# Reloading one batch in another layout, and reordering the start of an attention-plus-Fourier kernel

## The chip, the cores and the metric

The kernel runs on one core of a Trainium2 chip, as one launch. The metric is the device time of that launch in microseconds (us), and the number before is the median of seven executions.

## The reference

For each of 8 batches and 8 heads, 512 rows of `x` and 32 rows of `state` (64 wide) attend to each other. The 544 result rows of a batch, heads side by side (512 wide), then go through a two-dimensional Fourier mix of which only the real part is kept, a normalisation, a two-layer network (512 to 2048 to 512, relu) and a residual:

```python
a  = softmax(scale * x @ state.T);   xread = a @ state      # 512 rows per head
a2 = softmax(scale * state @ x.T);   sread = a2 @ x         # 32 rows per head
x  = concat([xread, sread]) as (8, 544, 512)
u  = x + real(fft(fft(x, axis=1), axis=2))
un = (u - mean(u)) / sqrt(var(u) + 1e-6)
out = u + relu(un @ w_ch1) @ w_ch2
```

## The kernel before

**Stages.** Each batch passes through four stages, each of which is a list of small steps (Python closures that issue instructions when called). `attend(b)` gives the scores (TensorE matmuls into tiles `eTp` and `esp`, ScalarE exps into `ET` and `E`) and then the reads (`xrp`, `xfp`, `xlp`, `srp`), which VectorE divides into `XR`, `XF`, `XL` and folds into `XQ`. `transform(b)` is the Fourier mix as matmuls with cosine and sine tables (`gp`, then `yp`), the sum `U`, its statistics, the centred `ub` and its transpose `unT`. `layer1(b)` multiplies with `w1` into `ph` and applies relu into `hT`; for batch 0 it works in quarter steps L[0] to L[15], of which L[0] to L[3] use the first 128 columns of `unT` and one quarter of `w1` each. `layer2(b)` multiplies with `w2` into `po` and writes the output.

**Who sets the order.** The program order of all engines is written out by hand: what is called first is issued first, and each engine works through its own queue. The first batch and part of the second stand in an explicit list (lines 818 to 830 before the change); after that, `weave` (line 797) merges the step lists of a stage by a fractional position, given as (list, start, end) for each. Between the steps at the start stand dummy matmuls: `warm(n)` (line 806) issues n 128x128 matmuls of the identity with itself, and `warmed(steps, n)` puts n of them behind each step.

**Loads.** `load_x(b)` fills the tile `xs` (two buffers). For batches 0 and 1 (line 112) partition p holds rows 4p to 4p+3 of every head, four rows of 64 floats in one run of 1,024 bytes: "four-row packets". Other batches are loaded row by row, 256 bytes each, in six DMAs on SyncE's (SP's) queue (lines 122 to 130), one of which has 31 partitions and one a single partition. The row order differs between the two layouts, so batches 0 and 1 undo the four-row interleave in `scores_t` (line 413) with strided matmuls: 18 for each of two head groups. `cast_x(b)` turns `xs` into the bf16 tile `xin`. For batches 0 and 1 TensorE transposes `xin` into `xT`; for later ones the DMA engines do it.

The weights are loaded by GpSimd's (POOL's) queue: `w1` behind a small copy into `gate` that waits for batch 0's x (lines 300 to 302), `w2` in `last_loads` (line 323). `more_loads` (line 309) stands in the list of batch 0's transform: it waits for batch 0's `XQ`, casts batch 1's x, then at line 312 reads `xs` of batch 0 and the last quarter of `w1`, and only then are a state reversal in DRAM, the load of batch 2's x and the clears for odd batches (`clears(1)`) in line. `clears(i)` (line 288) zeroes the pad columns of `XF`, `XR` and `XL` and some other tiles.

The explicit list of the second part reads, as far as the change touches it:

```python
for step in (warmed(t0[:2], 2) + [alternate, more_loads] + warmed(t0[2:4], 2) + [last_sines, exp_again, last_loads, turned[2], load_x3,
        t0[4], t0[8], W(6), turns1, t0[5], W(10), t0[7], copies1[0], copies1[1], t0[6], copies1[2],
        L[0], s1[0], t0[9], L[1], t0[10], s1[1], L[2], t0[11], t0[12], L[3], s1[2], r1[0], L[4], s1[3],
```

Here `t0` are the steps of `transform(0)`, `s1` and `r1` the scores and reads of batch 1, `s1[0]` and `s1[1]` its `scores_t`, `turns1` its transposes and `copies1` the copies of those out of PSUM. `t0[9]` transposes `ub` (0,0), `t0[10]` makes `ub` (1,1) on ScalarE, and `t0[12]` transposes that one.

Of the kernel before, what the change touches and what calls it, by code (L numbers as in the profile page):

```python
# [30 lines left out]
def kernel(  # L31
# [8 lines left out]
    nc = tc.nc  # L40
    B, H, S, D = x.shape
# [7 lines left out]
    NM = 288  # L49
# [59 lines left out]
    def load_x(b):  # L109
        xs = wk.tile([128, 4 * dm], F32, name="xs", tag="xs")  # L110
        xs_of[b] = xs
        if b < 2:
            v = xs.rearrange("p (h r) -> p h r", h=H)
            xb = x[b].rearrange("h (p i) d -> p h (i d)", i=4)
            n = 2 if b == 0 else 4
            for h in range(0, H, n):
                queue = nc.scalar if b == 0 and h in (0, 4) else nc.sync
                queue.dma_start(out=v[:, h:h + n, :], in_=xb[:, h:h + n, :])
            return
        v = xs.rearrange("p (i h d) -> p i h d", i=4, d=D)  # L120
        xb = x[b].rearrange("h s d -> s h d")
        for ps, si, rows in (
            (slice(32, 128), 2, xb[288:384]),
            (slice(0, 128), 0, xb[1:129]),
            (slice(0, 128), 1, xb[129:257]),
            (slice(0, 128), 3, xb[384:512]),
            (slice(0, 31), 2, xb[257:288]),
            (slice(31, 32), 2, xb[0:1]),
        ):
            nc.sync.dma_start(out=v[ps, si], in_=rows)  # L130

    def cast_x(b, copy=nc.gpsimd.tensor_copy, lo=0, hi=H):
        if b < 2:
            copy(xin_bufs[b % 2][:, :, 1 + D * lo:1 + D * hi].rearrange("p i (h d) -> p h i d", d=D),
                 xs_of[b].rearrange("p (h i d) -> p h i d", i=4, d=D)[:, lo:hi])
        else:
            copy(xin_bufs[b % 2][:, :, 1:513], xs_of[b].rearrange("p (i c) -> p i c", i=4))  # L137

    load_state(0, 1)
    load_x(0)  # L140
    load_state(1, 2)
    load_x(1)


    def turn_in_dram(lo, hi):
        nc.sync.dma_start(out=s_dram[lo:hi].rearrange("b h j d -> (b h) j d"),
                          in_=state[lo:hi, :, ::-1, :].rearrange("b h j d -> (b h) j d"))
# [137 lines left out]
            nc.gpsimd.memset(TO[0:1, lo:lo + 256:2], -v)  # L285
            nc.gpsimd.memset(TO[0:1, lo + 1:lo + 256:2], v)

    def clears(i):
        nc.gpsimd.memset(XFs[i][:, :, 512:514], 0.0)
        nc.gpsimd.memset(XRs[i][:, :, 0:514:513], 0.0)  # L290
        nc.gpsimd.memset(XLs[i][:, 512:514], 0.0)
        if i == 0:
            nc.gpsimd.memset(XE[:, 2, :], 0.0)
            nc.gpsimd.memset(XO[:, 2, :], 0.0)
            nc.gpsimd.memset(XO[:, 0:2, 0:257:256], 0.0)
        nc.gpsimd.memset(XNs[i].rearrange("p a b -> p (a b)"), 0.0)

    nc.gpsimd.tensor_copy(gate, xs_of[0][:, 0:2048:512])  # L300
    for q in range(4):
        nc.gpsimd.dma_start(out=w1[:, :, q * 512:(q + 1) * 512], in_=w1v[:, :, q * 512:(q + 1) * 512])
# [6 lines left out]
    def more_loads():  # L309
        nc.gpsimd.tensor_copy(gate[:, 0:1], XQs[0][:, 3, 0, 0:1])  # L310
        cast_x(1)
        nc.gpsimd.tensor_tensor(gate, xs_of[0][:, 0:4], w1[:, :, 3 * 512], op=ALU.add)
        turn_in_dram(3, B)
        load_x(2)
        clears(1)
        nc.gpsimd.memset(stb[:, 2:].rearrange("p b g c -> p (b g c)").bitcast(F32), 0.0)
# [10 lines left out]
    def qt(name, dt=F32):  # L327
        return psQ.tile([128, 512 if dt == F32 else 1024], dt, name=name, tag="q")
# [29 lines left out]
    def attend(b):  # L358
# [6 lines left out]
        sT = wk.tile([128, 4, 128], BF16, name="sT", tag="sT")  # L365
        xT = wk.tile([128, 4, S], BF16, name="xT", tag="xT")
# [45 lines left out]

        def scores_t(g):
            p = qt("eTp")
            for i in range(4):
                x0 = 128 * i
                for cols, rows in ((slice((i - 1) % 4, 285 if i == 0 else 288, 4), slice(x0 + (i == 0), x0 + 72)),
                                   (slice(287, 288), slice(0, 1)) if i == 0 else (None, None),
                                   (slice(291 - i, S, 4), slice(x0 + 127, x0 + 71, -1))):
                    for hp in range(2 if cols else 0):  # L420
                        nc.tensor.matmul(p[:, cols], lhsT=sT[:, 2 * g + hp, :], rhs=xT[:, 2 * g + hp, rows],  # L421
                                         start=(hp == 0), stop=(hp == 1))
            nc.scalar.activation(ET[:, g, :], p, AF.Exp, scale=scale)


# [286 lines left out]
    def layer1(key):  # L712
        low = isinstance(key, tuple)
        n = 128 if low else 512
        hT = wk.tile([128, FC, n], BF16, name="hTL" if low else "hT", tag="hTL" if low else "hT", bufs=1 if low else 2)
        h_of[key] = hT
        per = 512 // n

        def step(i):
            ph = psF.tile([128, 512], F32, name="ph", tag="c")  # L720
            for f in range(per * i, per * i + per):
                o = (f % per) * n
                for c in range(DC):
                    nc.tensor.matmul(ph[:, o:o + n], lhsT=w1[:, c, f * 128:(f + 1) * 128], rhs=un_of[key][:, c, :],  # L724
                                     start=(c == 0), stop=(c == DC - 1))
            nc.scalar.activation(hT[:, per * i:per * i + per, :].rearrange("p a b -> p (a b)"), ph, AF.Relu,  # L726
                                 scale=-1.0 if key in flipped else 1.0)

        def quarter_step(i, r):
            ph = psF.tile([128, 512], F32, name="ph", tag="c")  # L730
            for f in range(4 * i, 4 * i + 4):
                o = 128 * (f % 4)
                for c in range(DC):
                    nc.tensor.matmul(ph[:, o:o + 128], lhsT=w1[:, c, f * 128:(f + 1) * 128],  # L734
                                     rhs=un_of[key][:, c, 128 * r:128 * r + 128], start=(c == 0), stop=(c == DC - 1))
            nc.scalar.activation(hT[:, 4 * i:4 * i + 4, 128 * r:128 * r + 128], ph.rearrange("p (a b) -> p a b", b=128),  # L736
                                 AF.Relu, scale=-1.0 if key in flipped else 1.0)

        if key == 0:
            return [lambda i=i, r=r: quarter_step(i, r) for r in range(4) for i in range(FC // 4)]  # L740
        return [lambda i=i: step(i) for i in range(FC // per)]
# [69 lines left out]
    def warmed(steps, n):  # L811
        return [lambda s=s: (s(), warm(n)) for s in steps if s is not None]

    warm(12)
    s0, r0 = attend(0)
    s1, reads_next = attend(1)
    t0 = transform(0)
    for step in warmed(s0[:1], 8) + warmed(s0[1:2], 6) + warmed(s0[2:3], 14) + [second_table] + warmed(s0[3:5], 4) + s0[5:]:
        step()
    weave((warmed(r0, 4), 0, 1), ([sines], 0.25, 0.25), ([more_sines], 0.3, 0.3), ([lambda: warm(44)], 1, 1))  # L820
    load_x3 = lambda: (load_state(3, B, s_dram), load_x(3))
# [1 line left out]
    L, M, r1, t1 = layer1(0), layer2(0), reads_next, transform(1)  # L823
    W = lambda n: (lambda: warm(n))
    turns1, copies1, s1 = s1[0], s1[1:4], s1[4:]
    for step in (warmed(t0[:2], 2) + [alternate, more_loads] + warmed(t0[2:4], 2) + [last_sines, exp_again, last_loads, turned[2], load_x3,
            t0[4], t0[8], W(6), turns1, t0[5], W(10), t0[7], copies1[0], copies1[1], t0[6], copies1[2],
            L[0], s1[0], t0[9], L[1], t0[10], s1[1], L[2], t0[11], t0[12], L[3], s1[2], r1[0], L[4], s1[3],
            r1[2], t0[13], L[5], r1[1], L[6], r1[3], L[7], r1[4], r1[5], L[8], r1[7],
            lambda: state_ones(2, B), lambda: [r() for r in first_roots], L[9], L[10]]):  # L830
        step()
# [3 lines left out]
    for b in range(1, B + 1):  # L835
        reads_next = reads_after
        l2, l2_now = (layer2(b), l2[10:]) if b == 1 else (layer2(b) if b < B else [], l2)
        streams = [(l2_now + (layer2(("L", b // 4)) if b in (3, 7) else []), 0, 1)]
        if b < B:
            streams.append((layer1(b), 0.13 if b == 2 else 0.08, 1))  # L840
        if b + 1 < B:
            streams.append((reads_next, 0, 0.34))
            streams.append((transform(b + 1), 0.47 if b == 1 else 0.4, 0.77 if b == 3 else 0.8))
        if b + 2 < B:
            scores_next, reads_after = attend(b + 2)
            streams.append(([lambda: (cast_x(b + 2), turned[b + 2]())], 0.2, 0.2))
            streams.append((scores_next, 0.5, 1))
        if b + 3 < B:
            streams.append(([lambda: load_x(b + 3)], 0.35, 0.35))
        if b in (3, 7):  # L850
            streams.append((low_rows(b // 4), 0.02, 0.2))
            streams.append((layer1(("L", b // 4)), 0.36, 0.8))
        weave(*streams)
# [30 lines left out]
```

The softmax here doesn't subtract the row's maximum and nothing guards it: scores larger than these inputs give would overflow.

## Time and profile before

| what | value |
|---|---|
| time, median of 7 runs (lowest to highest) | 313.33 us (313.14 to 313.9) |
| the profiled execution: its time, its span | 313.23 us, 311.5 us |
| TensorE matmul, busy | 298.2 us, 96% of the span |
| VectorE, busy | 184.1 us, 59% |
| ScalarE, busy | 135.0 us, 43% |
| GpSimd, busy | 73.3 us, 24% |
| dummy matmuls (`warm`, line 809), busy | 12.6 us, 144 of them |
| scores of batches 0 and 1 (`eTp`, line 421), share of the chain | 1% |
| batch x loads of 256 KB on SP, median from issue to landing | 4.7 us |
| weight loads of 512 KB on GpSimd's queue, median from issue to landing | 11.2 us |

How to read it: in the lines of the profile PE is TensorE's matmuls, PEld its weight loads, DVE VectorE, ACT ScalarE, POOL GpSimd and SP SyncE. An L with a number is a line of the kernel before. "Busy" counts dummies as work, so TensorE's share says how little it pauses, not how much of its work is needed. Matmul ends are modelled, so the distance from one start to the next is the surer measure. Idle time in brackets names what ended it.

### The profile page before, as it was taken

To read this page: it belongs to the slowest core of one execution; us is meant where nothing else is said; L and a number is where in the kernel's file an instruction comes from. 1 tells how busy PE (TensorE), PEld (TensorE's weight loads), DVE (VectorE), ACT (ScalarE), POOL (GpSimd) and SP (SyncE) were. 2 spreads that over 40 slices of the span, in tenths; PEclk is the share of its full clock that TensorE was granted. 3 is DMA by queue.
4 is the path that set the end of the run, shared out by engine and by line. 5 is a ranking of instruction groups with operands and counts; after the bars stand their busy time and mean duration, and the time that the engine had idled before them with its cause. 6 is when DMAs were issued, how large, how long until landed. Compare 5 with 4: busy or idle time off the path is not lost.

```text
span 311.5 us, 5999 instructions
## 1 busy us (share of the span) xinstructions
PE 298.2 (96%) x2316; PEld 172.6 (55%) x2348; DVE 184.1 (59%) x441; ACT 135.0 (43%) x265; POOL 73.3 (24%) x168
## 2 busy tenths in 40 slices
PE   5988999999999999999999999999999999999995
PEld 5867996544544545456545554455445544555443
DVE  8787782786878484864727684686469563100112
ACT  5598674736533443244533435244424333333300
POOL 5969590540240040301500024002200131000000
PEclk9999999999999999999999999999999999999999
DMA  7997999159255756267533579631333034303055
GB/s 243 196 182 134 176 149 203 44 120 190 48 116 96 145 104 136 71 115 122 136 95 54 128 122 163 135 86 51 85 70 67 36 83 97 76 34 67 36 131 138
DMA packets 108052, 34.86 MB, mean 112 GB/s; under 512 B 97400, under 2 KB 103800, under 8 KB 108024
## 3 DMA queue, kind: packets, MB, share of 16 engines
q1 hardware_dynamic: 98840, 28.72, 45.3%
q0 software_dynamic: 4224, 4.19, 8.5%
q10 hardware_dynamic: 4960, 1.57, 2.1%
q8 instruction: 18, 0.29, 0.4%
q14 instruction: 10, 0.08, 0.1%
HBM read 22.41 MB, written 14.02 MB: 117 GB/s over the span
## 4 chain that ended last, share of the span: by engine, by line
PE 82%; DVE 13%; issue 2%; ACT 2%; POOL 1%; DVEq 0%; POOLq 0%; ACTq 0%
PE po L789 32%; PE ph L724 30%; PE gp L599 4%; PE ph L734 3%; DVE U L569 2%; DVE st L335 2%; PE warm L809 1%; PE eTp L421 1%; PE po L781 1%; PE yp L565 1%; PE xfp L457 1%; PE xrp L457 1%; PE yp L564 1%; PE gp L603 1%; PE esp L432 1%
## 5 line engine op out<-in xcount | busy, mean ns | idle before, releaser
L789 PE MATMUL po<-w,hT 128*128 128x512 bf16 x476 | 122.0, 379 | 1.5 <-issue 0.8
L726 ACT ACTIVATE hT<-ph 128x512 bf16<-128x512 f32 x112 | 66.9, 597 | 124.8 <-PE ph L724 122.7
L724 PE MATMUL ph<-unT,w 128*128 128x512 bf16 x437 | 114.0, 379 | 1.0 <-DVE ot L755 0.3
L724 PEld LDWEIGHTS <-w 128*128 128x128 bf16 x576 | 51.1, 98 | 47.9 <-issue 0.8
L789 PEld LDWEIGHTS <-hT 128*128 128x128 bf16 x496 | 47.1, 98 | 45.3
L755 DVE SCALAR_TENSOR_TENSOR ot<-po,rstd,U 128x512 f32<-128x512 f32 (+2 forms) x33 | 24.2, 732 | 52.8 <-PE po L789 44.9
L609 POOL COPY GL<-G 128x128 bf16<-128x128 bf16 x8 | 2.3, 291 | 113.7 <-ACT G L607 113.7
L569 DVE TENSOR_TENSOR U<-yp,XR 128x512 f32<-128x512 f32 x16 | 10.9, 682 | 27.0 <-PE yp L565 27.0
L335 DVE BATCH_NORM_STATS2 st<-U 128x6 f32<-128x512 f32 x32 | 21.8, 682 | 0.1
L342 POOL TENSOR_TENSOR rstd<-rstd,mhalf 128x1 f32<-128x1 f32 x34 | 21.0, 619 | 2.7
L341 POOL TENSOR_TENSOR rstd<-mv,epst 128x1 f32<-128x1 f32 x34 | 6.8, 200 | 62.5 <-DVE mv L337 62.5
L607 ACT CAST G<-gp 128x288 bf16<-128x288 f32 x31 | 12.1, 397 | 10.7 <-PE gp L603 5.7
L734 PE MATMUL ph<-unT,w 128*128 128x128 bf16 x256 | 16.1, 219 | 0.5 <-ACT unT L645 0.5
L809 PE MATMUL warm<-ident 128*128 128x128 bf16 x144 | 12.6, 236 | 3.7 <-POOL ident masks.py:199 3.3
L734 PEld LDWEIGHTS <-w 128*128 128x128 bf16 x256 | 15.0, 98 | 0.8 <-issue 0.6
L599 PEld LDWEIGHTS <-XQ 128*128 128x128 bf16 x96 | 8.8, 98 | 8.8 <-DVE XQ L529 2.5
L809 PEld LDWEIGHTS <-ident 128*128 128x128 bf16 x144 | 10.5, 107 | 4.6 <-POOL ident masks.py:199 3.3
L633 DVE TENSOR_SCALAR ub<-U,mv 128x512 bf16<-128x512 f32 x24 | 12.2, 510 | 1.3 <-DVE mv L337 0.5
L137 POOL CAST xin<-xs 128x2048 bf16<-128x2048 f32 x6 | 11.3, 1889 | 3.5 <-PE tp L642 3.5
L457 PEld LDWEIGHTS <-ET 128*128 128x128 bf16 x80 | 7.0, 98 | 9.1 <-DVE XF L466 1.8
L466 DVE TENSOR_TENSOR XR<-xrp,rs 128x512 bf16<-128x512 f32 x16 | 11.1, 695 | 0.8 <-POOL XR L290 0.2
L736 ACT ACTIVATE hT<-ph 128x512 bf16<-128x512 f32 x16 | 9.4, 598 | 4.2 <-PE ph L734 4.0
(183 smaller groups left out, 352.4 us busy)
## 6 DMA issues: line engine op xcount, KB each, us to landing
xs<-in_x_dram SPq DMA_DIRECT2D x20, 256.0 KB, 4.7
w<-in_moe_w_ch_dram POOLq DMA_DIRECT2D x8, 512.0 KB, 11.2
out_dram<-ot SPq DMA_DIRECT2D x15, 256.0 KB, 3.5
r_dram<-ot SPq DMA_DIRECT2D x14, 256.0 KB
out_dram<-r_dram SPq DMA_DIRECT2D x14, 256.0 KB, 3.7
xs<-in_x_dram SPq DMA_DIRECT2D x6, 192.0 KB
xs<-in_x_dram SPq DMA_DIRECT2D x2, 512.0 KB
xs<-in_x_dram ACTq DMA_DIRECT2D x2, 256.0 KB
```

The lines of the kernel that those rows point to most:

```text
L335: nc.vector.bn_stats(st6, u)
L342: nc.gpsimd.tensor_tensor(rstd, rstd, mhalf, op=ALU.pow)
L457: nc.tensor.matmul(ph[:, 0:260], lhsT=ET[:, g, c0:c0 + 128], rhs=rhs, start=True, stop=True)
L569: nc.vector.tensor_add(u.rearrange("p (k r) -> p k r", r=2), p.rearrange("p (r k) -> p k r", r=2)[:, 0:u.shape[1] // 2, :], x.rearrange("p ...
L599: nc.tensor.matmul(p[:, 0:NM], lhsT=XQ[:, j, c, :], rhs=tab[c], start=(c == 0), stop=(c == 2 and j != 2))
L633: nc.vector.tensor_scalar(t, in0=ud, scalar1=mv[:, 0:1], scalar2=None, op0=ALU.subtract)
L724: nc.tensor.matmul(ph[:, o:o + n], lhsT=w1[:, c, f * 128:(f + 1) * 128], rhs=un_of[key][:, c, :], start=(c == 0), stop=(c == DC - 1))
L726: nc.scalar.activation(hT[:, per * i:per * i + per, :].rearrange("p a b -> p (a b)"), ph, AF.Relu, scale=-1.0 if key in flipped else 1.0)
L734: nc.tensor.matmul(ph[:, o:o + 128], lhsT=w1[:, c, f * 128:(f + 1) * 128], rhs=un_of[key][:, c, 128 * r:128 * r + 128], start=(c == 0), st ...
L755: nc.vector.scalar_tensor_tensor(ot[:, cols], in0=po_of[i][:, 0:cols.stop - cols.start], scalar=rstd, in1=u[:, cols], op0=ALU.mult, op1=AL ...
L789: nc.tensor.matmul(po_of[i], lhsT=h_of[key][:, f, i * 128:(i + 1) * 128], rhs=w2[:, f, :], start=(f == 0), stop=(f == FC - 1))
L809: nc.tensor.matmul(t[:, 0:128], lhsT=ident, rhs=ident, start=(i == 0), stop=(i == n - 1))
```

## The change

Six edits. Only batch 0 keeps the four-row packets; batch 1's x is loaded, cast and scored in the plain row layout, which makes its `scores_t` four matmuls a group (two of 288 columns and two of 224). The dummies in batch 0's turns and scores become fewer: 6 to 4, 14 to 0, and twice 4 to 0. The pad clears leave `clears` for a function `pads` of their own, called ahead of the gate and trigger of `w1` (batch 0's), and ahead of the read of `w1`'s last quarter (batch 1's). L[1] is issued ahead of batch 1's first scores. Layer 1 of batches 3 and 7 starts at 0.1 of its stage instead of 0.08, and `transform(2)` at 0.5 instead of 0.47.

```diff
     def load_x(b):
...
-        if b < 2:
+        if b == 0:
             v = xs.rearrange("p (h r) -> p h r", h=H)
             xb = x[b].rearrange("h (p i) d -> p h (i d)", i=4)
-            n = 2 if b == 0 else 4
-            for h in range(0, H, n):
-                queue = nc.scalar if b == 0 and h in (0, 4) else nc.sync
-                queue.dma_start(out=v[:, h:h + n, :], in_=xb[:, h:h + n, :])
+            for h in range(0, H, 2):
+                queue = nc.scalar if h in (0, 4) else nc.sync
+                queue.dma_start(out=v[:, h:h + 2, :], in_=xb[:, h:h + 2, :])
             return
...
     def cast_x(b, copy=nc.gpsimd.tensor_copy, lo=0, hi=H):
-        if b < 2:
+        if b == 0:
...
-    def clears(i):
+    def pads(i):
         nc.gpsimd.memset(XFs[i][:, :, 512:514], 0.0)
         nc.gpsimd.memset(XRs[i][:, :, 0:514:513], 0.0)
         nc.gpsimd.memset(XLs[i][:, 512:514], 0.0)
+
+    def clears(i):
...
+    pads(0)
     nc.gpsimd.tensor_copy(gate, xs_of[0][:, 0:2048:512])
...
     def more_loads():
         nc.gpsimd.tensor_copy(gate[:, 0:1], XQs[0][:, 3, 0, 0:1])
         cast_x(1)
+        pads(1)
         nc.gpsimd.tensor_tensor(gate, xs_of[0][:, 0:4], w1[:, :, 3 * 512], op=ALU.add)
...
         def scores_t(g):
             p = qt("eTp")
+            if b == 1:
+                for lo, hi, src in ((0, NM, slice(0, NM)), (NM, S, slice(S - 1, NM - 1, -1))):
+                    for hp in range(2):
+                        nc.tensor.matmul(p[:, lo:hi], lhsT=sT[:, 2 * g + hp, :], rhs=xT[:, 2 * g + hp, src],
+                                         start=(hp == 0), stop=(hp == 1))
+            else:
...
-    for step in warmed(s0[:1], 8) + warmed(s0[1:2], 6) + warmed(s0[2:3], 14) + [second_table] + warmed(s0[3:5], 4) + s0[5:]:
+    for step in warmed(s0[:1], 8) + warmed(s0[1:2], 4) + [s0[2], second_table] + s0[3:]:
...
-            L[0], s1[0], t0[9], L[1], t0[10], s1[1], L[2], t0[11], t0[12], L[3], s1[2], r1[0], L[4], s1[3],
+            L[0], L[1], s1[0], t0[9], t0[10], s1[1], L[2], t0[11], t0[12], L[3], s1[2], r1[0], L[4], s1[3],
...
-            streams.append((layer1(b), 0.13 if b == 2 else 0.08, 1))
+            streams.append((layer1(b), 0.13 if b == 2 else 0.1 if b in (3, 7) else 0.08, 1))
...
-            streams.append((transform(b + 1), 0.47 if b == 1 else 0.4, 0.77 if b == 3 else 0.8))
+            streams.append((transform(b + 1), 0.5 if b == 1 else 0.4, 0.77 if b == 3 else 0.8))
```

## The prediction

> **What bounds the kernel now.** I read the page first, its busy shares.
>
> ```profile
> PE 298.2 (96%) x2316; PEld 172.6 (55%) x2348; DVE 184.1 (59%) x441; ACT 135.0 (43%) x265; POOL 73.3 (24%) x168
> ```
>
> TensorE (PE) is the bound from about 42 us on, where its waits are 0.3 us or less. Only the time before leaves room, and "busy" hides waste there: dummies (tile `warm`) count as PE work. So I then asked for the chain of waits between 3 and 50 us (start, length, what).
>
> ```profile
> 8.08 0.78 PE warm L809 x14
> 8.86 0.94 PE eTp L421 x18
> 9.80 0.22 PE warm L809 x4
> 10.03 0.96 PE eTp L421 x18
> ...
> 13.96 0.21 DVE rs L465
> ...
> 27.85 0.92 ACT xT L407
> 28.78 0.04 issue
> 28.82 1.10 PE eTp L421 x18
> ...
> 31.04 0.94 PE eTp L421 x18
> 31.98 0.89 PE ph L734 x16
> 32.87 0.22 PE tp L642 x4
> 33.10 0.89 PE ph L734 x16
> ...
> 41.91 6.25 PE ph L734 x112
> ```
>
> Two dummy blocks lie on the chain (0.78 and 0.22 us). From 14 to 23 us the chain is VectorE (DVE), without a pause, so whatever comes earlier at 13.96 arrives earlier at 26. Batch 1's scores (eTp, 28.82 and 31.04) are on it too, after a wait for ScalarE's (ACT) copy of xT. From 41.91 PE runs unbroken: time won ahead of it is kept to the end.
>
> The timeline adds four rows (start, length, engine, operation; in brackets the idle time and its cause):
>
> ```profile
> 12.51 0.70 DVE L466 TENSOR_TENSOR XR<-xrp,rs 128x512 bf16<-128x512 f32 x1 [0.21 <-POOL XR L290]
> 27.62 4.30 SPq L130 DMA_DIRECT2D xs<-in_x_dram  x1
> 31.57 0.71 ACT L631 ACTIVATE ub<-U,mv 128x512 bf16<-128x512 f32 x1
> 73.34 0.42 PE L599 MATMUL gp<-CT,XQ 128*128 128x288 bf16 x2 [0.32 <-DVE XQ L529]
> ```
>
> **What the Trainium skill says.** "TensorE: Matmul & The Clock Gate", Part 1, says PE starts at half clock and gets the full clock after about 3.4 us of sustained activity, in a window that does not start with the kernel. The trace agrees in kind: eight 128x128 transposes took 1.06 us at 5.96 and 0.63 us at 7.45. The same page (architectural detail) calls ACT's and DVE's queues strictly first in, first out; the order of ACT's rows below matters for that. "DMA: Bandwidth & Descriptors", Specifications, puts the least size for full rate at 512 B; in its part on why a DMA adds 16 to its semaphore, it says a piece of 127 partitions falls on one DMA engine, as no larger number up to 16 divides it. By that rule the 31-row piece of x lands on one engine. The trace fits: the last issue of batch 2's x, behind that piece, held SP 4.30 us, the first 0.36 us.
>
> **The change, part by part.** Times in the order before to after.
>
> *Dummies.* 24 go: 2 ahead of the second transposes of x, 14 ahead of the first scores, 4 behind each score. The 14: their 0.78 us goes, but scores then wait for ACT's xT copy (7.06 + 1.01 = 8.07), so they start at about 8.12 instead of 8.86. The 4 between save 0.22. The second scores need DVE's xT copy (8.81), which is in time. They end at 8.12 + 0.94 + 0.96 = 10.0, against 10.99: 0.95 won. The last 4 lie beside ACT's exp: nothing. The 2 let the transposes start at 7.35, held by POOL's cast: nothing on the chain.
>
> *Does the 0.95 arrive at DVE?* Its first reciprocal moves from 12.09 to 11.3, limited by the second table's rows (end 11.31). There the 0.21 wait for the pads of XR falls away, so the XR write ends near 12.25 instead of 13.21. The reciprocal at 13.96 comes at about 13.0. Two covers thin out: POOL's part of the fold ends at 18.57 now and moves only 0.36, since its state casts end at 14.60, while DVE's XQ wants to start at 18.2; and ACT's sines end at 21.63 minus about 0.9. Both fit by a hair. I take **0.85**; ends 0.5 and 0.95.
>
> *Pads.* Three POOL memsets (0.1 us each, 0.03 apart) go ahead of the weights' trigger at 7.45: w1 starts 0.1 to 0.2 us later, and the clears behind them end no later. Layer 1 first reads w1 at 27.14. Zero on the chain.
>
> *Batch 1's scores.* 2 x 18 narrow matmuls become 2 x 4 (288 and 224 columns). Six 128x288 gp matmuls advance the chain 0.73 us at 48.16, 0.12 each; four take 0.46 or less. Per group the next block starts 0.92 us later now (28.82 to 29.74; 30.88 to 31.80): 2 x 0.46 = 0.92 of PE saved. L[1] ahead of s1[0] also fills the 0.47 us for which PE waited for xT. PE alone would win 1.4.
>
> *What is late next.* ACT. Its queue becomes: relu L[0], relu L[1], exp, unT copy, ub of (1,1). From relu L[0] (29.25 now) the spacings in the trace are 0.53 (three relus at 40.44 take 1.58), 0.53, 0.49, 0.62: ub starts at 31.4 and ends at 32.1, less the 0.85. Its transposes (0.41 with the start-up, as at 26.28) release L[3] at 32.5 - 0.85 = 31.65, against 33.10. So beyond the 0.85 only **0.6** of the 1.4 comes through; ends 0.2 and 1.4. DVE's next read (34.48) was bound by PE, and DVE's own rows end at 33.61 - 0.85, so it follows.
>
> *Batch 1's x.* SP issues six DMAs for two, in 256 B packets. Price: batch 2's x. In the windows:
>
> ```profile
> 10.00:23.00 13.00, 11.33 (x154) 9.38 (x152) 9.97 (x32) 11.47 (x29) 9.63 (x32) 1.00 1.15 190
> 25.00:31.00 6.00, 4.96 (x82) 4.43 (x80) 4.17 (x11) 5.04 (x10) 5.78 (x12) 1.00 0.98 174
> ```
>
> (The last two columns are DMA share and GB/s.) That load used 6 us at share 0.98, 5.9 us of all engines; batch 1's, at 329 GB/s and share 1.08 from 5 to 9, about 3.4. So 2.5 us more DMA work stands ahead of w1, which fills 10 to 23 (share 1.15): w1's last quarter lands near 25.5 instead of 23.3, and later if the one-engine piece holds it. Layer 1 needs that quarter at L[3] (33.10): covered. But POOL's gate on it (L312, 24.03, no wait now) stalls 2 us or more. Behind it: batch 2's x (SP), table copies, the w2 trigger (28.96), stb, the cast of batch 2's x (36.88). Who waits: batch 2's scores at 52.86, whose xT transposes were issued by 44.7 (5 us ahead), and w2's first use at 48.73. The pads of XR1 (read at 34.79) now stand ahead of the gate. Zero, until the stall passes 3.5 us. SP's own queue: the state reversals slip by the six issues (up to 8 us); their first reader is POOL's stb cast at 31.96. Zero. The cast of batch 1 reads one straight run instead of strides: 1.95 to about 1.89 us, beside DVE's chain. Zero.
>
> *Weave.* transform(2) starts at 0.5 instead of 0.47 of its stage: one block later, so the 0.32 us at 73.34 should go. Layer 1 of batches 3 and 7 starts 0.02 later: nothing waits there that it would cure. Taken 0.2, ends -0.3 and 0.5 (order changes can open waits as well).
>
> **Sum.** 0.85 + 0.6 + 0.2 = 1.65 us. The profiled execution took 313.23 (span 311.5 and 1.7 around it), 0.1 below the median of 313.33. 313.33 - 1.65 = **311.7 us**; ends 1.3 below nothing lost (0.5 + 0.2 - 0.3 = 0.4, 312.9) and 2.85 (310.5).
>
> **Rivals.**
> - *Only one half comes through* (0.18): ACT (sines, then the exp queue) or DVE sets the pace and the scores' saving turns into PE waits. For it: ACT is 0.9 busy from 14 to 23 us. Gain 0.5 to 0.9, 312.6.
> - *Batch 1's x lands too late* (0.10), the slower side. POOL wants it at 21.2 in the new order; PE needs the cast (1.95) by about 23.5, so lateness past 21.6 costs one for one. Worked from batch 2: first issue 24.09, last queue hold to 31.92, plus a landing of 4.7 gives 12.5 us; from 2.77, and 3 us behind batch 0's x, it lands at 18. Against: 3 us in hand. For: w1's packets share the engine with the 31-row piece, which no row shows alone. It decides from 23.9 on (1.65 + 0.63 past 21.6); at 24.5 the time is 314.6.
> - *The clock comes late* (0.05): with two dummies fewer PE idles 0.1 us at 7.25; were that to cost one more 3.4 us window, 44 score and transpose matmuls would take about 0.05 us more each, 2.2 in all: 313.9.
> - *The later weaves lose what was won* (0.05): 313.3.
> - *Main case* 0.62: 311.7, own range 310.7 to 312.6.
>
> About 0.2%, 0.6 us, is what a measurement of this kernel can tell from no change. Faster by more: 0.62 plus two thirds of the first rival, 0.74; within: 0.12; slower: 0.14. The range 310.8 to 313.5 leaves out the slow ends and the best case.
>
> **What would show it.** Right: eTp at about 8.1 and near 9.1; no wait for XR's pads; XQ near 18.3; L[3] near 31.7 behind a PE wait of 0.5 to 0.9 us for ub; POOL waiting at its gate; the unbroken stretch of layer 1 starting near 40.5. Wrong: narrow-matmul rates as before 7.4 still at 9 us (clock), a POOL cast of batch 1 behind a DMA wait (late x), a PE wait at batch 2's scores (late weights and x), or new PE waits past 60 us.

## The result, and the profile after

The changed kernel takes **317.77 us** (median of 12 runs, 315.57 to 320.07), the kernel before, run beside it, 313.42 us (31 runs): a ratio of 1.0137, 95% interval 1.0116 to 1.0159. It is slower by 4.35 us where 1.65 us were to be won. The profiled execution took 316.96 us with a span of 315.2, 3.7 more than before's 311.5.

The page, first the busy times, then the granted TensorE clock in 40 slices of 7.9 us, then the shares of the chain by engine (the chain is the work that ended last, followed back from wait to wait; a q behind an engine's name is its queue, which waits and issues):

```profile
PE 297.5 (94%) x2264; PEld 171.4 (54%) x2296; DVE 184.9 (59%) x441; ACT 135.1 (43%) x265; POOL 73.7 (23%) x168
PEclk9997999999999999999999999999999999999999
PE 70%; DVE 15%; DMA 7%; issue 2%; ACT 2%; SPq 1%; POOL 1%; DVEq 0%; POOLq 0%; ACTq 0%
```

TensorE has 52 matmuls fewer and is busy 0.7 us less, but its share falls from 96 to 94%: the span has holes. A DMA now holds 7% of the chain. The clock dips in the fourth slice (24 to 32 us). So I read the chain of waits there (start, length, what):

```profile
7.99 16.48 DMA xs<-in_x_dram
...
25.11 1.91 POOL xin L136
...
27.06 1.32 PE xTp L404 x16
...
33.00 0.97 ACT hT L745 x2
33.98 0.50 ACT ET L432
...
34.52 0.60 PE eTp L421 x4
...
45.03 6.25 PE ph L743 x112
```

The chain before ran through VectorE from 14 to 23 us. Now one load of x covers 8 to 24.5 us, then come POOL's cast and the transposes of it. The unbroken stretch of layer 1 starts at 45.03 instead of 41.91: 3.1 us of the 3.7 are lost by then. The timeline gives the waits (single rows of it: start, length, engine, operation, in brackets the idle time before it and what ended it):

```profile
2.77 11.37 SPq L129 DMA_DIRECT2D xs<-in_x_dram  x6
8.13 2.04 PE L430 MATMUL eTp<-xT,sT 128*128 128x71 bf16 x36 [0.27 <-ACT xT L396]
11.62 0.70 DVE L475 TENSOR_TENSOR XR<-xrp,rs 128x512 bf16<-128x512 f32 x1
25.11 1.90 POOL L136 CAST xin<-xs 128x2048 bf16<-128x2048 f32 x1 [3.55 <-DMA xs<-in_x_dram]
27.06 1.32 PE L404 MATMUL xTp<-ident,xin 128*128 128x128 bf16 x16 [3.17 <-POOL xin L136]
```

Rows two and three are the start as forecast: scores at 8.13, and the write of XR without its wait for the pads. Row one is batch 1's x: its six issues hold SP until 14.14. Rows four and five are the loss. POOL stands 3.55 us for x and TensorE then 3.17 us for POOL; before, those transposes started at 24.33 without a wait.

VectorE's instructions come in the same order in all kernels here, so the start of each can be set against its start in the kernel before. For the changed kernel this shift is -0.80 us at 13.96, -0.61 at 27, **+3.13 at 34.5**, +3.13 at 73, +3.23 at 80, +3.57 at 92.5 and +3.96 at 131 and at the end. So there are three losses: 3.7 us at batch 1's x, 0.4 us between 73 and 93 (0.1 at 79, 0.34 at 92), and 0.4 us between 126 and 131. "Shift" below means this.

### The profile page after: what moved, and what is told of

Same layout as the page of the kernel before. It is cut to its first block, busy times and chain, and to the rows that moved or that the text cites. A ratio compares the mean times of both kernels' runs of the same rounds, so it can differ in the third digit from the quotient of the medians.

```text
span 315.2 us, 5901 instructions
## 1 busy us (share of the span) xinstructions
PE 297.5 (94%) x2264; PEld 171.4 (54%) x2296; DVE 184.9 (59%) x441; ACT 135.1 (43%) x265; POOL 73.7 (23%) x168
## 4 chain that ended last, share of the span: by engine, by line
PE 70%; DVE 15%; DMA 7%; issue 2%; ACT 2%; SPq 1%; POOL 1%; DVEq 0%; POOLq 0%; ACTq 0%
PE po L798 29%; PE ph L733 26%; DMA xs<-in_x_dram 6%; PE ph L743 3%; PE gp L608 3%; DVE U L578 3%; DVE st L338 3%; DVE ot L764 1%; SPq L129 1%; DMA unT<-ub 1%; DVE ub L642 1%; PE po L790 1%; PE xrp L466 1%; PE xfp L466 1%; DVE XF L475 1%
## 5 line engine op out<-in xcount | busy, mean ns | idle before, releaser
L136 POOL CAST xin<-xs 128x2048 bf16<-128x2048 f32 x7 | 13.2, 1891 | 8.3 <-PE ph L743 4.7
L818 PE MATMUL warm<-ident 128*128 128x128 bf16 x120 | 11.1, 245 | 3.7 <-POOL ident masks.py:199 3.3
L818 PEld LDWEIGHTS <-ident 128*128 128x128 bf16 x120 | 9.4, 112 | 4.6 <-POOL ident masks.py:199 3.3
```

What stands on the lines that cost most here:

```text
L818: nc.tensor.matmul(t[:, 0:128], lhsT=ident, rhs=ident, start=(i == 0), stop=(i == n - 1))
```

## The experiments

The theory after this reading: the 31-row piece of batch 1's x, on one DMA engine, is slowed by `w1` there; TensorE waits, its clock falls, and the rest of the change brings less than forecast. The rivals: the new order or the strided scores cost the time, or the clock alone, or the weaves.

**All of the change but the layout.** Batch 1's x stays in four-row packets, its scores strided.

```diff
-        if b == 0:
+        if b < 2:
...
-            if b == 1:
+            if b < 0:
```

> The changed kernel with batch 1's x put back into four-row packets (load, cast and strided scores as before); everything else of the change stays. Theory A (the row layout's one-partition-group piece lands late behind the weights, and nothing else is lost): the whole loss goes and the rest of the change wins 0.6 to 1.3 us, 312.1 to 312.8 us; the cast of batch 1 starts near 21.5 us without a DMA wait. Rival B (fewer dummies or the new order cost the time themselves): it stays above 315 us.

Measured: 313.39 us, ratio 0.9997 (0.9986 to 1.0008). Without the new layout the loss is gone, so it is the layout's. But the rest of the change brings nothing either: the shift is -0.61 at 34.5, and only -0.14 at the end, since 0.1 goes at 79 us and 0.4 between 126 and 131, where the weave numbers act.

**The layout alone**, put into the kernel before.

```diff
-        if b < 2:
+        if b == 0:
...
+            if b == 1:
+                for lo, hi, src in ((0, NM, slice(0, NM)), (NM, S, slice(S - 1, NM - 1, -1))):
```

> The kernel before with only batch 1's x in the row layout (load, cast, four score matmuls a group). Theory A: the x lands near 24.5 us as in the changed kernel, the cast waits for it, and the time is 316.5 to 319 us, since the prefix is not even earlier. Rival B: within 0.6 us of 313.4, since the layout is not what costs.

Measured: 315.93 us, ratio 1.0080 (1.0044 to 1.0116), in runs from 314.23 to 318.3. The layout alone makes the kernel slower, although its scores are cheaper. Its profile fell on a short execution (span 312.7), in which POOL waited 1.80 us for x and TensorE 1.69 us. The changed kernel varies as much (over 4.5 us). Two things differ from one execution to the next: when x lands (the cast starts at 24.21 here, at 25.11 in the changed kernel's trace), and the mean granted clock, 1.0 in the fastest executions of both kernels and 0.988 to 0.995 in the slower ones.

**The one-engine piece cut in two**, for batch 1 alone, 16 rows and 15.

```diff
-            (slice(0, 31), 2, xb[257:288]),
+            *([(slice(0, 16), 2, xb[257:273]), (slice(16, 31), 2, xb[273:288])] if b == 1 else [(slice(0, 31), 2, xb[257:288])]),
```

> The changed kernel with the 31-row piece of batch 1's x cut into 16 and 15 rows, so that it spreads over 16 and 15 DMA engines instead of one; as many 256 B packets as before. Theory A1 (one engine holds the piece back): batch 1's x lands by 13 us, no wait of POOL's cast, 311.8 to 312.7 us. Rival A2 (small packets as such are slow beside the weights): the x still lands after 20 us and the time stays above 315 us.

Measured: **312.85 us**, ratio 0.9977 (0.9970 to 0.9985). Its timeline, the cast, the transposes and the second scores of batch 1:

```profile
22.20 1.90 POOL L136 CAST xin<-xs 128x2048 bf16<-128x2048 f32 x1 [0.43 <-DMA gen<-s_dram]
24.15 1.07 PE L404 MATMUL xTp<-ident,xin 128*128 128x128 bf16 x16
30.50 0.60 PE L421 MATMUL eTp<-xT,sT 128*128 128x288 bf16 x4 [0.98 <-ACT ET L432]
```

One line of a load makes the difference of 4.9 us. The cast starts 2.9 us earlier, and the transposes run at full clock (1.07 us against 1.32). Same bytes, same packets, same SP queue: it is the piece on one engine, and not the packets' size as such, that was late. The 0.43 us ahead of the cast are no wait for x, whose packets end before 18 us: with `w1` moved (last experiment) x has landed by 15 us and the gap is 0.42. With four-row packets there is none: in the first experiment the cast starts at 21.47, right behind POOL's copy ahead of it.

The third row shows the bound that the prediction had foreseen. The second scores wait for ScalarE's exp, 0.98 us. The shift is -0.88 at 34.5, against -0.39 at 27 in that execution: the four wide matmuls bring 0.49 us, where 0.6 was forecast.

**Why the piece is late: the DMA view.** In the trace of the changed kernel, 22 to 25 us, by queue (q0 carries `w1`, q1 SP's loads; the last figure is the share of 16 engines):

```profile
DMA packets 61, 0.05 MB, mean 18 GB/s; under 512 B 31, under 2 KB 60, under 8 KB 60
q0 software_dynamic: 30, 0.03, 5.8%
q8 instruction: 1, 0.02, 2.5%
q1 hardware_dynamic: 30, 0.01, 1.9%
```

Hardly anything else moves; 5.8% of 16 is 0.93 of one engine, so this fits one busy engine that carries 30 packets of each queue in 3 us. They take turns, one for one, and since a packet of `w1` takes about 96 ns, x gets 10 packets per us. From 13 to 17 us it is the same: 39 packets of SP's loads in 4 us beside 801 of `w1`. Alone, such a piece makes 61 per us, as the view of the last experiment shows. The Trainium skill states this in "DMA: Bandwidth & Descriptors", Queues, rings and completion order: each DMA engine takes turns between the queues it has work for, a packet at a time. The prediction had used that page's rule on the number of engines and not this one. At 10 per us 248 packets (31 rows by 8 heads) would take 25 us, at 61 they take 4.

**The clock.** 54 more dummies are put ahead of batch 1's transposes, where TensorE waits.

```diff
-            t0[4], t0[8], W(6), turns1, t0[5], W(10), t0[7], copies1[0], copies1[1], t0[6], copies1[2],
+            t0[4], t0[8], W(60), turns1, t0[5], W(10), t0[7], copies1[0], copies1[1], t0[6], copies1[2],
```

> The changed kernel with 60 dummies instead of 6 ahead of batch 1's transposes, which fill most of the 3.2 us for which PE waits for the cast. Theory: part of the loss is the half clock that follows the wait (27.7 to 31.1 us in the record of the changed kernel); with PE kept busy the clock stays full and 0.5 to 1.2 us come back, 316.6 to 317.3 against a median of 317.8, with a narrower spread. Rival (the clock costs nothing, since ScalarE is what PE meets next): the same 317.8 or more.

Measured: 316.46 us, ratio 1.0099 (1.0067 to 1.0130). The stretch from 27.7 to 31.2 us, in the changed kernel and then with the dummies (busy time and count of PE, PEld, DVE, ACT, POOL, then granted clock, DMA share, GB/s):

```profile
27.70:31.20 3.50, 3.04 (x31) 2.81 (x29) 0.00 (x0) 0.87 (x3) 3.34 (x7) 0.51 0.70 159
```

```profile
27.70:31.20 3.50, 3.04 (x52) 2.77 (x49) 0.42 (x1) 2.51 (x5) 3.34 (x8) 1.00 0.69 156
```

PE is busy 3.04 us in both and finishes 31 matmuls in one, 52 in the other: a clock of 0.51 against 1.00. The records put the half clock at 27.73 to 31.14, 3.4 us, after the wait of 3.17 us. "TensorE: Matmul & The Clock Gate", Part 1, says an idle window of about 3.4 us brings the half clock; here a slightly shorter pause was enough.

Between the medians lie 1.3 us. In the traces x was cast 1.05 us earlier with the dummies, but TensorE started on it only 0.47 earlier (26.59), being busy with them; the shift at 34.5 is 1.64 us better, so about 1.2 us is the clock's. The two ratio intervals overlap slightly, so the size is less sure than the mechanism. For the mechanism speaks that the mean granted clock was 1.000 in all four executions with the dummies, and in only one of twelve of the changed kernel. It doesn't explain the spread alone: with a clock of 1.000 the four still reach from 314.99 to 317.46 us.

**Weave numbers alone**, each put into the kernel before. First layer 1 of batches 3 and 7:

```diff
-            streams.append((layer1(b), 0.13 if b == 2 else 0.08, 1))
+            streams.append((layer1(b), 0.13 if b == 2 else 0.1 if b in (3, 7) else 0.08, 1))
```

> The kernel before with only layer 1 of batches 3 and 7 starting at 0.1. Theory (it takes a matmul block from between batch 4's reads, so that PE waits for DVE there): slower by 0.3 to 0.5 us, 313.7 to 313.9. Rival (harmless by itself): 313.2 to 313.5.

Measured: 313.85 us, ratio 1.0010 (1.0001 to 1.0019), a loss of 0.3. In its trace the shift is +1.2 from 8 us on already (batch 0's x was cast late in that execution), and it grows by 0.4 us between 126 and 131, as in the changed kernel. One block of layer 1 has left the reads of batch 4, and TensorE waits between them for VectorE to empty their PSUM tiles, for instance 0.2 us at `xfp` behind the write of XL. With the start edits too, a single weight load waits 0.7 us there.

Then the transform of batch 2:

```diff
-            streams.append((transform(b + 1), 0.47 if b == 1 else 0.4, 0.77 if b == 3 else 0.8))
+            streams.append((transform(b + 1), 0.5 if b == 1 else 0.4, 0.77 if b == 3 else 0.8))
```

> The kernel before with only transform(2) starting at 0.5 instead of 0.47. The prediction gave it 0.2 us of gain (the 0.32 us wait of PE for XQ at 73.34 us goes). Rival, from the trace of the changed kernel: that wait goes, but the gp blocks stand closer together and PE waits 0.2 us each for XQ and for G; then 313.3 to 313.5, no gain.

Measured: 313.66 us, ratio 1.0001 (0.9991 to 1.0011). TensorE's waits from 70 to 95 us (engine, line, waited for; us in total, times, longest):

```profile
PE gp L599 <- DVE XQ L533: 0.2, 1, 0.2
PE yp L565 <- ACT G L607: 0.2, 1, 0.2
```

The wait of 0.32 us that the prediction wanted gone is gone; these two stand in its place, and the shift grows by 0.1 at 79.

**The cut piece with the weaves of before.**

```diff
-            (slice(0, 31), 2, xb[257:288]),
+            *([(slice(0, 16), 2, xb[257:273]), (slice(16, 31), 2, xb[273:288])] if b == 1 else [(slice(0, 31), 2, xb[257:288])]),
...
-            streams.append((layer1(b), 0.13 if b == 2 else 0.1 if b in (3, 7) else 0.08, 1))
+            streams.append((layer1(b), 0.13 if b == 2 else 0.08, 1))
```

(and 0.47 for the transform.)

> The run with the 31-row piece cut in two (312.85 us), with the three weave numbers of the kernel before (layer 1 at 0.08 in batches 3 and 7, transform(2) at 0.47). In its trace the lead over the kernel before is 0.89 us at 73 us, 0.78 at 80 and falls from 1.06 to 0.20 between 126 and 147 us, where the weave numbers act. Theory (the weave numbers cost the lead): 312.1 to 312.5 us, and the lead stays near 0.8 us to the end. Rival (the lead is lost to something else that comes with being early, such as transposes by DMA): 312.7 to 313.0.

Measured: 312.82 us, ratio 0.9974 (0.9960 to 0.9988). That can't be told from the 0.9977 with the new weaves. In the traces the 0.4 us at 126 to 131 is absent here, but 0.4 is lost between 80 and 92 instead: TensorE waits 0.25 us for a transpose of `ub` by the DMA engines (`unT` of batch 2) at 90.57. That wait also stands in the changed kernel (the shift's step of 0.34 there), and not in the kernel before. It comes with the layout: a step of 0.2 to 0.6 us at 92 stands in seven of the eight traces with batch 1's x in rows (all but the one with more dummies), and in none of the five others with four-row packets, the start edits alone among them, which are 0.7 us early. By which path is not shown.

**The small pieces first.** If the piece on one engine is late, issue it ahead of the four large pieces.

```diff
+        small = [(slice(0, 31), 2, xb[257:288]), (slice(31, 32), 2, xb[0:1])]
...
+            *(small if b == 1 else []),
...
```

> The changed kernel with batch 1's 31-row piece (and the single row) issued ahead of its four large pieces, still on one DMA engine and still in 256 B packets. Theory (the piece is slow only because it meets w1's packets on its engine and takes turns with them, about 9 to 10 packets a us from 11 us on): it runs ahead of w1, batch 1's x lands by 15 us, POOL's cast doesn't wait, 312.6 to 313.3 us. Rival (248 small packets on one engine are slow whatever runs beside them): still above 315 us.

Measured: 319.74 us, ratio 1.0193 (1.0172 to 1.0214). My theory had expected a cure and was wrong. The timeline and, below it, the DMA queues from 11 to 22 us:

```profile
2.76 16.30 SPq L130 DMA_DIRECT2D xs<-in_x_dram  x6
27.50 1.90 POOL L137 CAST xin<-xs 128x2048 bf16<-128x2048 f32 x1 [5.53 <-DMA xs<-in_x_dram]
```

```profile
q0 software_dynamic: 1702, 1.69, 90.5%
q1 hardware_dynamic: 1797, 0.45, 30.6%
```

The piece itself ran at about 67 packets per us from 6 to 8 us. But SP's later issues queued behind it, the last one ending at 19.06, and so the other 3,840 packets of x met `w1` on all engines, one for one: 1,797 to 1,702 in 11 us. Taking turns counts packets and not bytes, so a load in 256 B packets gets a fifth of the bytes beside one in 1,024 B. TensorE waits 5.15 us for the cast in this execution, and the records put the half clock at 26.53 to 33.35, 6.8 us.

**The start edits alone**: dummies and pads, in the kernel before.

```diff
...
+    pads(0)
...
+        pads(1)
...
-    for step in warmed(s0[:1], 8) + warmed(s0[1:2], 6) + warmed(s0[2:3], 14) + [second_table] + warmed(s0[3:5], 4) + s0[5:]:
+    for step in warmed(s0[:1], 8) + warmed(s0[1:2], 4) + [s0[2], second_table] + s0[3:]:
```

> The kernel before with only the fewer dummies and the earlier pad clears (both batches). Prediction's term: 0.85 us of lead. The changed kernel's trace has 0.80 at 13.96 us but 0.61 from 20 us on, since the folds of DVE and POOL slow each other. Theory (0.6 arrives at PE and stays): 312.7 to 312.9 us. Rival (ScalarE or DVE takes it back in batch 1's scores): 313.2 to 313.5.

Measured: **312.84 us**, ratio 0.9980 (0.9971 to 0.9989). Shift -0.89 at 13.96, and -0.70 from 27 to the end. Before 27, at 17 to 18 us, lies the loss between the two. The sum Sm and the fold of XE behind it, before and then in this kernel:

```profile
17.57 0.67 POOL L519 TENSOR_TENSOR XE<-Sm 128x256 f32<-128x256 bf16 x1
17.93 0.60 DVE L518 TENSOR_TENSOR Sm<-XF,XR 128x514 bf16<-128x514 bf16 x1
18.56 0.43 DVE L519 TENSOR_TENSOR XE<-Sm 128x256 f32<-128x256 bf16 x1
```

```profile
17.05 0.43 DVE L522 TENSOR_TENSOR Sm<-XF,XR 128x514 bf16<-128x514 bf16 x1
17.13 0.87 POOL L523 TENSOR_TENSOR XE<-Sm 128x256 f32<-128x256 bf16 x1
17.51 0.78 DVE L523 TENSOR_TENSOR XE<-Sm 128x256 f32<-128x256 bf16 x1
```

Before, DVE's half of XE began after POOL's had ended, but its Sm began inside it. Now Sm begins first and DVE's half of XE inside POOL's. XE takes 0.35 us longer on DVE and 0.20 on POOL, Sm 0.17 less; for DVE that is 0.18 in all, the loss in the lead. In each of these overlaps the one that begins later is the one that takes longer. "SBUF — State Buffer", Who interferes with whom, says that a VectorE instruction with two SBUF inputs contends with a GpSimd one that reads SBUF. The trace agrees with the page in that the overlap costs, 0.17 to 0.35 us here.

**The cut for every batch**, with the weaves of before.

```diff
-            (slice(0, 31), 2, xb[257:288]),
+            (slice(0, 16), 2, xb[257:273]),
+            (slice(16, 31), 2, xb[273:288]),
```

> The run with the old weave numbers and the cut piece (312.82 us), with the 31-row piece cut into 16 and 15 rows for all batches from 1 on. Theory (one engine's queue holds SP 4.3 us at the end of each load, and the transposes of unT stand behind it on SP): the last issue falls under 1 us, the 0.25 us wait of PE for unT at 90.6 us shrinks, 312.3 to 312.8. Rival (no transfer of x is late for batches from 2 on, so nothing moves): 312.6 to 313.1.

Measured: 313.88 us, ratio 0.9994 (0.9977 to 1.0011). Nothing more is won, and the trace gives back 0.64 us between 80 and 93 us, again at `unT` of batch 2 (shift -0.69 at 34.5, -0.05 at 92.5).

**The order alone**, L[1] ahead of s1[0] in the kernel before.

```diff
-            L[0], s1[0], t0[9], L[1], t0[10], s1[1], L[2], t0[11], t0[12], L[3], s1[2], r1[0], L[4], s1[3],
+            L[0], L[1], s1[0], t0[9], t0[10], s1[1], L[2], t0[11], t0[12], L[3], s1[2], r1[0], L[4], s1[3],
```

> The kernel before with only L[1] issued ahead of batch 1's first scores (strided scores, four-row packets). Theory (PE's 0.5 us wait for xT is filled, but ScalarE gets one more relu ahead of its exp and its ub, and PE waits for that instead): within 0.2 us of 313.4. Rival (the wait goes for good): 312.8 to 313.0.

Measured: 313.27 us, ratio 1.0001 (0.9984 to 1.0019); shift +0.04. The order is free and worth nothing by itself: the second scores wait for ScalarE's exp.

**`w1` behind x.** In the changed kernel the four triggers of `w1` move behind POOL's state casts.

```diff
-    for q in range(4):
-        nc.gpsimd.dma_start(out=w1[:, :, q * 512:(q + 1) * 512], in_=w1v[:, :, q * 512:(q + 1) * 512])
...
+    for q in range(4):
+        nc.gpsimd.dma_start(out=w1[:, :, q * 512:(q + 1) * 512], in_=w1v[:, :, q * 512:(q + 1) * 512])
```

> The changed kernel with w1's four DMAs issued on POOL behind the constants, clears and state casts instead of ahead of them: about 3.5 us later, POOL's work in the same sum. The 31-row piece stays on one engine. Theory (the piece lands late only because it takes turns with w1's packets): it is through at about 66 packets a us before w1's packets come near 13.5 us; batch 1's x lands by 15 us, POOL's cast doesn't wait, 312.6 to 313.4 us, though w1 itself lands 4 us later. Rival (the piece is slow for another reason, or the later w1 holds layer 1 up): above 315 us.

Measured: 316.49 us, ratio 1.0120 (1.0060 to 1.0180), from four executions between 315.55 and 319.62. The trace is that of the fastest; the two slowest had a granted clock of 0.995 and 0.989, and what more they lost isn't shown. The first half went as the theory said. SP's queue alone, 11 to 13 us, on its piece:

```profile
q1 hardware_dynamic: 122, 0.03, 8.4%
```

That is 61 packets per us, and the cast (22.47) does not wait for x. The second half is a loss that the prediction had costed at nothing. The timeline:

```profile
26.93 0.20 POOL L315 TENSOR_TENSOR gate<-xs,w 128x4 f32<-128x4 f32 x1 [2.44 <-DMA w<-in_moe_w_ch_dram]
31.17 0.42 POOL L261 COPY SL<-gen 32x288 bf16<-32x288 bf16 x1
31.63 1.08 ACT L745 ACTIVATE hT<-ph 128x512 bf16<-128x512 f32 x2 [2.36 <-POOL SL L261]
```

POOL stands 2.44 us at its gate on the last quarter of `w1`, so the copies of the table ends behind it (into CL and SL) finish at 31.6. ScalarE's first relu of batch 0 waits 2.36 us for the last of them, since the source of those copies (`gen1`, where `cl1` and `sl1` lie) is a buffer of the tag `hT` (tiles of one tag use the same buffers in turn), which that relu writes. TensorE's next scores then wait 3.5 us for ScalarE. The shift goes from -0.11 at 27 to +1.87 at 34.5.

## Why the prediction was wrong, step by step

The failed step is **"from 2.77, and 3 us behind batch 0's x, it lands at 18", with "3 us in hand"**. It scaled the load of batch 2, whose one-engine piece ran at about 60 packets per us. Batch 1's piece ran at 40 to 45 from 11 to 13 us and, where it can be seen alone in its queue, at 9 to 11 after that (13 to 17 and 22 to 24 us), and x landed at 24.46. The rival "Batch 1's x lands too late" named this mechanism, its place and its reason (`w1`'s packets share the engine with the piece), but got 0.10. (That its example of 24.5 met the landing is luck: no sum of it leads there.) It deserved more: 11 us of `w1` lay in plain view across the landing estimate. The one case of such a piece beside other packets, batch 2's beside `w2` before, showed it undisturbed, but for 3 us only.

That rival priced a landing at 24.5 with 314.6, and 317.77 came out (316.96 in the profiled execution). It left out four things: the 0.65 us from the landing to the cast's start, the half clock after TensorE's pause (about 1.2 us), the 0.4 us that the weave of layer 1 costs, and the 0.4 us up to 93, of which 0.34 lies at `unT`. Together they are 2.65 us, a little more than the 2.36 that the profiled execution took beyond 314.6; the clock's part is the least sure.

The other steps:

- *Dummies and pads*: the place and the mechanism were right (scores at 8.13 for 8.12, no wait for XR's pads). Mis-sized: 0.85 came out as 0.61 in the changed kernel's trace and 0.70 in that of the start edits alone, whose ratio stands for 0.35 to 0.9. One of the two covers that "fit by a hair" did not fit: DVE's part of the fold now begins inside POOL's.
- *Clock at the start*: right for the changed kernel's trace, where the full clock comes at 7.25 us (7.48 before). But its place moves between executions, from 6.0 to 9.5 us in the traces of this case, and where it came latest the sign that the prediction named did show: with the small pieces first, the 36 score matmuls took 2.65 us from 8.14 on instead of 2.04, and the shift at 13.96 was -0.18 only. In the traces with the start edits that shift is -0.75 to -0.95 where the full clock came before 7.9 us, and -0.18 to -0.59 where it came after 8.4. Whether fewer dummies make a late clock more frequent is open: of the five traces without these edits, the latest had it at 8.24.
- *Batch 1's scores*: right in kind, ScalarE is next, and 0.6 came out as 0.49 where x was in time. TensorE's wait is for the exp (0.98 us) and not for `ub`: the exp stands behind two relus in ScalarE's queue.
- *Weave*: +0.2 was forecast. The transform's number gave nothing, layer 1's cost 0.3. "Nothing waits there that it would cure" was right and should have led to a price below zero.
- *POOL's gate*: "Zero, until the stall passes 3.5 us" was wrong: a stall of 2.44 us, with `w1` moved, was not free. The stall of 2 us or more that was forecast did not come in the changed kernel, nor with the cut piece, where POOL passes the gate at 24.16 without a wait. I asked who waits for the casts and triggers behind the gate, and took the table copies for harmless because their readers come late. Their source buffer is what is waited for. In the changed kernel this cost can't be told from x, since relus there end up behind the late cast anyway; with `w1` moved it stands alone, 2.4 us at the relu.
- *Sum*: even with x in time the change brings 0.5 to 0.8 us (312.8 to 312.9 us with the cut piece) and not 1.65. That is the number of "Only one half comes through", but not its mechanism: the scores' saving arrived (0.49), and the weave numbers (0.1 and 0.4 in the trace) and the step at 92 (0.2) took it back. The start edits alone give as much (312.84 us). The three versions that beat both kernels, the start edits and the two with the cut piece, can't be told apart.

What stays open: why the piece was not slowed to 10 packets per us from the first packet of `w1` on, but only some 3 us later. The same holds for batch 2's piece, which keeps 60 per us through the first 3 us of `w2` (30.5 to 33.5 us before, 182 packets) and is then nearly through. The trace does not name the DMA engine of a packet; that the piece sits on one is inferred from the rule that the prediction cites, the 0.93 of an engine above and the cure by 16 and 15 rows. Also open is why the DMA transposes come late near 92 us with the row layout.

## What to carry to other kernels

Before a load is re-cut, look up how many DMA engines each piece gets and what else is queued on them at that time: a rate seen alone is no price beside another queue, since turns go by packets. A piece of 31 rows is better cut in 16 and 15, and only where it competes. When a stall is declared free, follow not only the readers of what stands behind it but also the buffers that it keeps occupied; and if TensorE is to pause about 3 us, add the half clock to the price.

## What the runs showed of the hardware

- Two DMA queues share the engines packet for packet: 30 to 30 in 3 us where one engine's worth was moved, 1,797 to 1,702 in 11 us on all, with 256 B against 1,024 B. For the piece on one engine this began only about 3 us after the second queue's first packet.
- A pause of 3.17 us of TensorE brought 3.4 us of half clock, which cost about 1.2 us, and one of 5.15 us brought 6.8 us; one of 1.69 us (the layout alone) brought none.
- The full clock at the start came between 6.0 and 9.5 us in fourteen traces whose first matmuls all start near 3.3 us.
- Two folds of 128x256 bf16 to f32, on VectorE and GpSimd at the same time, took 0.78 and 0.87 us instead of 0.43 and 0.67. POOL's had begun inside a DVE instruction, and DVE's inside POOL's; neither waited for the other's end.
